# A convolution, norm and FFN kernel: interleaved partitions, another weight path, smaller first parts, a new order

## The chip, the cores and the metric

One core of a Trainium2 chip. The metric is the device time of one execution in microseconds; 921.21 us is the median of 3 runs of the kernel before (921.13 to 921.22).

## The reference

For x of 8 x 4224 x 192 and gate logits of 8 x 4224 x 8 x 7 (batch, position, head, tap):

```python
w = softmax(weight_gen, axis=-1)                        # 7 taps per head
x_unf = the 7 positions s-6 .. s of x, zeros before position 0
out = einsum('bshk,bskhg->bshg', w, x_unf)              # 24 channels per head
xn = (out - mean) / sqrt(var + 1e-6) * g_ln             # over 192 channels
result = out + maximum(xn @ w_ch1, 0) @ w_ch2           # 192 -> 768 -> 192
```

w_ch1 and w_ch2 arrive as float64; the other inputs and the result are float32.

## The kernel before

The 8 x 4224 positions are cut into 128 runs of 264; a partition holds one run, partition p the run p in order, so a batch takes 16 neighbouring partitions. A "token" is one column, 128 positions at once, and t runs from 0 to 263. The taps of the first six tokens need the six positions before the run: `load_x` (L277) fetches them into the columns 0 to 5 of the x buffer with one transfer for each batch (L286), and the first partition of each batch keeps zeros (L234). x lives in a ring of 36 columns.

Work goes by *parts* (`PARTS`, L21: three of 4 tokens, twenty of 12, then 8 and 4), cut into *chunks* of 4 or 6 tokens. For a part, `softmax` (L303) makes the tap weights in PSUM (wn). For a chunk, `conv` (L350) has VectorE multiply x by the weights (L382): three instructions with two taps each into pr, one with one tap into y. Two accumulating transfers issued by GpSimd (L388) and four GpSimd additions (L385) sum the taps; in the first chunk VectorE adds instead. `norm` (L416) has ScalarE make sums and squares of each token (L426, L431), the reciprocal root for the whole part (L454), five small VectorE steps (L459 to L465), and then for each *group* of four tokens the scaled activation (L477), its float16 high half (L484, ScalarE) and low half (L486, GpSimd), and a transposing transfer from SyncE's queue into xT (L490).

`products` (L494) takes a group. In each of three *hidden blocks* ten matmuls of 128x512 (L505) fill one ph in PSUM; ScalarE takes the Relu's high half (L514), VectorE its low half (L516). `output` (L525) makes the second product, 18 matmuls of 128x192 for each token (L537 to L539) into po, and VectorE adds two tokens to y (L550), which then goes out (L557). There are two each of ph, po, hh and hlo.

The weights come first. Their float64 words are loaded from SyncE's queue (L578; the last 64 rows of W1 twice, into both halves of the partitions). `from_double` (L592) joins two 32-bit words into a float32 with three VectorE steps (L611, L614, L617), through a second tile half in pr, and GpSimd flushes tiny values to zero (L621, L622). `w_scale` (L628) finds a power of two from the sum of squares through a matmul with ones (L633). W1 is scaled by g and split into a high and low float16 half; its last 64 rows and shifted copies lie in further blocks, copied by ScalarE (L683) and VectorE (L697). W2 is converted in two halves; its final scale is fs (L708), its halves are made at L714 (ScalarE) and L716 (GpSimd).

The order is planned ahead: each operation has an engine, an estimated cost and a due time in tokens (`WANT`, `W_WANT`, L29: so many tokens ahead of the group's turn on TensorE), and `Plan.order` (L88) places operations one after another on a model of the engines; it takes, among those that can start within `AHEAD` ns of the first, the one due first, and only those due within `WINDOW` tokens of the oldest open one. `FIRST` shifts the first 12 tokens. Each engine then works through its list in that fixed order, SyncE's and GpSimd's transfers included.

Of the kernel before, what the change touches and what calls it, by code (L numbers as in the profile page):

```python
# [20 lines left out]
PARTS = (4, 4, 4) + (12,) * 20 + (8, 4)  # L21
# [7 lines left out]
WANT = {'load': 30, 'wload': 43.75, 'max': 23.72, 'sub': 26.56, 'exp': 24.37, 'sum': 21.85,  # L29
    'rcp': 21.33, 'inv': 20.83, 'mul': 15.95, 'conv': 18.52, 'step': 0.9, 'dma': -0.4, 'add':  # L30
    0.61, 'sums': 6.45, 'squares': 6.1, 'rstd': 5.09, 'newton': 3, 'xh': 1.38, 'lo': 5.87}
W_WANT = {'load': 38.65, 'a': 20.41, 'c': 19.78, 's1': 14.01, 'load2': 16.96, 'c2': 6.55, 's2':
    5.13}
FIRST = {'soft': 1.35, 'conv': -1.66, 'norm': 6.53}
AHEAD = 57.45
WINDOW = 8
# [14 lines left out]
class Plan:  # L51


    DMA_START = {"SP": 1250.0, "Pool": 650.0}
# [101 lines left out]
def kernel(  # L156
# [21 lines left out]
    PMAX = max(PARTS)  # L178
    MMAX = PMAX * H
    assert sum(PARTS) == C and D == 192 and F == 6 * P and S == PB * C  # L180

# [11 lines left out]
    pool("w", 3, [P, PMAX, HK], F32)  # L193
# [35 lines left out]
    def dma_ns(n):  # L229
        return n * P / 350.0  # L230
# [3 lines left out]
    Q.memset(X[:, 0:PAD, :], 0.0)  # L234
# [8 lines left out]
    xsrc = xf.rearrange("(p t) d -> p t d", p=P)  # L243
    wsrc = wg.rearrange("b s h k -> (b s) (h k)").rearrange("(p t) f -> p t f", p=P)
    osrc = out.rearrange("b s d -> (b s) d").rearrange("(p t) d -> p t d", p=P)

    parts, chunks, s0 = [], [], 0
    for n in PARTS:
        pa = dict(S=s0, n=n, chunks=[], xT={})
        o = 0  # L250
        while o < n:
            m = min(CHUNK, n - o) if n % CHUNK == 0 else min(4, n - o)
            ch = dict(S=s0 + o, o=o, n=m, part=pa)
# [13 lines left out]
    def pieces(ch, k):  # L267

        t0, n = ch["S"], ch["n"]
        if t0 % RING == 0:  # L270
            return t0 % RING + k
        return xcol(t0) - PAD + k

    def sp(want, fn, r, w, dma):
        op("SP", 60, want, fn, r=r, w=w, dma=dma)

    def load_x(ch):  # L277
        t0, n = ch["S"], ch["n"]
        want = t0 - WANT["load"]
        if t0 == 0:  # L280

            def first():
                for b in range(B):
                    p = b * PB + 1
                    src = bass.AP(tensor=xf.tensor, offset=(p * C - PAD) * D, ap=[[C * D, PB - 1], [1, PAD * D]])
                    SY.dma_start(X[p : p + PB - 1, 0:PAD, :].rearrange("p t d -> p (t d)"), src)  # L286
            op("SP", 480, want, first, w=[("x", "h")], dma=dma_ns(PAD * D * 4))
        elif t0 % RING == 0:
            sp(want, lambda: SY.dma_start(X[:, 0:PAD, :], xsrc[:, t0 - PAD : t0, :]), [], [("x", "h")],
               dma_ns(PAD * D * 4))  # L290
# [125 lines left out]
    def norm(pa):  # L416
# [53 lines left out]
        for g in range(0, n, NT):  # L470
# [9 lines left out]
            for j in range(0, NT, 2):  # L480
# [10 lines left out]
               [(hl, 0), (hl, 1)], [xT], 2300.0)  # L491


    def products(pa, g, s, prev):  # L494
# [13 lines left out]
        for u in range(3):  # L508
# [3 lines left out]
            op("PE", 2160, su, lambda u=u, ph=ph: hidden(u, ph), [xT, "w1"], [ph])  # L512
# [12 lines left out]
    def output(gp, t, s):  # L525
# [28 lines left out]
        for ch in pa["chunks"]:  # L554
            if ch["y"] is y and j + 2 == ch["n"]:
                n, t0 = ch["n"], ch["S"]
                sp(s + 0.4, lambda: SY.dma_start(osrc[:, t0 : t0 + n, :], at(y)[:, :n, :]),  # L557
                   [(y, i) for i in range(n)], [], dma_ns(n * D * 4))
# [3 lines left out]
    for name, shape, dt in (("g", [P, 2], F32), ("gi", [P, 2], F32), ("s1", [P, 4], F32),  # L562
# [3 lines left out]
        W[name] = cp.tile(shape, dt, name="c_" + name)  # L566
    gcol = g_ln.rearrange("(d o) -> d o", o=1)
    hn = NF // 2 * D
# [6 lines left out]
    def load_weights():  # L575

        def dma(want, dst, src, n, w):
            op("SP", 60, -W_WANT[want], lambda: SY.dma_start(dst(), src), w=[w], dma=dma_ns(n))  # L578
# [5 lines left out]
        dma("load2", lambda: words(2, 0, 2 * NF * D).rearrange("p (j d) -> p j d", d=2 * D), wv2,  # L584
            8 * NF * D, raw[2])

    def load_g():
        A.dma_start(W["g"][:, 0:1], gcol[0:P, :])
        for h in (top, bot):
            A.dma_start(W["g"][h, 1:2], gcol[P:D, :])  # L590

    def from_double(want, src, dst, n, sq, r, w):  # L592


        m = Buf("pr")
        t = m
# [4 lines left out]
        def mv():  # L601
            return at(m)[:, 0].rearrange("p t d -> p (t d)")[:, :n]

        def tv():
            return at(t)[:, 1].bitcast(I32).rearrange("p t d -> p (t d)")[:, :n]

        want = -W_WANT[want]
        op("ACT", a_ns(n), want, lambda: A.activation(mv(), part(1).bitcast(F32), AF.Square), r, [(m, 0)])

        op("V", v_ns(n / 2), want,  # L610
           lambda: V.tensor_scalar(out=tv(), in0=part(1), scalar1=3, scalar2=0x3FFFFFFF,  # L611
                                   op0=ALU.logical_shift_left, op1=ALU.bitwise_and), r, [(t, 1)])
        op("V", v_ns(n), want,
           lambda: V.scalar_tensor_tensor(out=tv(), in0=part(0), scalar=29, in1=tv(),  # L614
                                          op0=ALU.logical_shift_right, op1=ALU.bitwise_or), r, [(t, 1)])
# [9 lines left out]
        op("ACT", a_ns(n, 186), want,  # L625
           lambda: A.activation(mv(), dst(), AF.Square, accum_out=sq), w, [(m, 0), (w[0], "sq")])
# [25 lines left out]
    def weights():  # L652
# [5 lines left out]
        def f32(b, n, o=0):  # L658
            if b is not w2r:
# [4 lines left out]
        from_double("c", lambda: words(1, 0, 2 * F), lambda: f32(wc, F), F, s1[:, 1:2],  # L664
                    [(raw[1], 0), (raw[1], 1)], [wc])
# [9 lines left out]
        op("V", 580, want, gsum, [(wa, "sq"), (wc, "sq")], ["s1"])  # L675
# [28 lines left out]
        op("V", 70, want2, lambda: V.tensor_tensor(out=s2[:, 2:3], in0=s2[:, 0:1], in1=s2[:, 1:2], op=ALU.add),  # L704
           [((w2r, 0), "sq"), ((w2r, 1), "sq")], ["s2"])
        w_scale("s2", s2[:, 2:3], 16384.0, r2, ["s2"], "r2")
# [4 lines left out]
        wv = [(w2r, 0), (w2r, 1)]  # L711
# [8 lines left out]
    load_g()  # L720
    for i, pa in enumerate(parts):
        load_w(pa)
# [5 lines left out]
        softmax(pa)  # L728
        for ch in pa["chunks"]:
            conv(chunks.index(ch))  # L730
# [39 lines left out]
```

## Time and profile before

| | |
|---|---|
| median of the runs | 921.21 us |
| profiled execution, its own time | 926.91 us |
| its span, first to last instruction | 925.1 us |
| busy share: TensorE, VectorE, ScalarE, GpSimd | 90%, 85%, 73%, 75% |
| mean granted TensorE clock | 0.989 |
| moved by transfers | 145.10 MB, 157 GB/s on average |

PE is TensorE, DVE is VectorE, ACT is ScalarE, POOL is GpSimd, SP is SyncE; a trailing q means the engine's queue, which also issues transfers. L12 is line 12 of the kernel. A timeline or chain row gives the start in us, the duration in us and what ran; a bracket gives the idle time before it and what ended it. The chain of waits is followed back from the last instruction.

### The profile page before, as it was taken

The page shows a single profiled execution, that of the slowest core. Times are in us where ns is not written, and L with a number is a line of the kernel's source. Part 1 is how long each engine was busy: PE and PEld are TensorE (multiplying, and loading weights), DVE is VectorE, ACT ScalarE, POOL GpSimd, SP SyncE. Part 2 cuts the span into 40 slices and gives each one's busy share as a digit, 9 for nine tenths or more (in the row PEclk, how much of TensorE's full clock was granted, in tenths as well). Part 3 has the DMA queues.
Part 4 walks back from the last instruction along what each step waited for, and adds up shares of the span by engine and source line. Part 5 has one row for each costly group of instructions (what it writes and reads, how often), then busy time and mean ns, then how long its engine had stood idle before and what let it go on. Part 6 is the DMA issues. An engine that isn't in the chain of part 4 may idle for free.

```text
span 925.1 us, 17424 instructions
## 1 busy us (share of the span) xinstructions
PE 831.6 (90%) x6736; PEld 588.4 (64%) x6736; DVE 790.6 (85%) x798; ACT 676.9 (73%) x1760; POOL 697.5 (75%) x378
## 2 busy tenths in 40 slices
PE   0025889999989999999999899999999999999998
PEld 0012647676767677777767677767776767777776
DVE  6989989988969889899898898988989889886432
ACT  2466779787777877968879578787796877878721
POOL 5688997977859788797887787978879688797200
PEclk9997989999999999999999999999999999999999
DMA  7446586798897898987987989889898798756311
GB/s 215 149 106 157 137 203 158 127 217 148 146 174 132 229 159 158 204 146 190 179 137 201 144 192 178 128 203 168 179 206 117 189 164 169 160 113 137 67 37 52
DMA packets 136018, 145.10 MB, mean 157 GB/s; under 512 B 107400, under 2 KB 108808, under 8 KB 135936
## 3 DMA queue, kind: packets, MB, share of 16 engines
q1 hardware_dynamic: 122672, 92.88, 44.6%
q0 software_dynamic: 12960, 51.12, 31.5%
q8 instruction: 52, 0.85, 0.4%
q14 instruction: 30, 0.25, 0.1%
q10 hardware_dynamic: 304, 0.00, 0.0%
HBM read 40.96 MB, written 25.95 MB: 72 GB/s over the span
## 4 chain that ended last, share of the span: by engine, by line
PE 64%; DVE 19%; DMA 7%; POOL 5%; issue 4%; ACT 1%; SPq 0%; DVEq 0%; POOLq 0%
PE ph L505 34%; PE po L539 10%; PE po L537 10%; PE po L538 10%; DVE pr L382 9%; DMA xT<-hl 6%; POOL y L385 4%; DVE hlo L516 3%; DVE y L382 2%; DVE y L550 1%; DMA hh<-in_moe_w_ch_dram 1%; POOL hl L486 1%; DVE y L385 1%; DVE pr L614 1%; DVE wn L343 1%
## 5 line engine op out<-in xcount | busy, mean ns | idle before, releaser
L385 POOL TENSOR_TENSOR y<-y,pr 128x1152 f32<-128x1152 f32 (+1 forms) x180 | 483.5, 2690 | 66.2 <-DVE pr L382 62.8
L505 PE MATMUL ph<-xT,c_w1h 128*128 128x512 f16 x1188 | 422.7, 384 | 53.8 <-DMA xT<-hl 43.5
L539 PE MATMUL po<-c_w2h,hlo 128*128 128x192 f16 x1584 | 389.8, 246 | 3.1 <-DVE hlo L516 3.1
L538 PE MATMUL po<-c_w2l,hh 128*128 128x192 f16 x1584 | 389.8, 246 | 0.7 <-POOL c_w2l L716 0.7
L537 PE MATMUL po<-c_w2h,hh 128*128 128x192 f16 x1584 | 389.8, 246 | 0.0
L382 DVE TENSOR_TENSOR pr<-x,wn 128x2304 f32<-128x2304 f32 (+1 forms) x138 | 334.8, 2439 | 2.8 <-POOL y L385 2.1
L514 ACT ACTIVATE hh<-ph 128x1024 f16<-128x1024 f32 x198 | 200.6, 1013 | 155.4 <-PE ph L505 155.4
L505 PE MATMUL ph<-xT,c_w1l 128*128 128x512 f16 x792 | 304.3, 384 | 0.0
L516 DVE SCALAR_TENSOR_TENSOR hlo<-ph,hh 128x1024 f16<-128x1024 f32 x198 | 240.6, 1216 | 60.7 <-ACT hh L514 60.6
L505 PEld LDWEIGHTS <-c_w1h 128*128 128x128 f16 x1188 | 117.6, 99 | 138.6 <-DMA xT<-hl 9.8
L486 POOL TENSOR_TENSOR hl<-xh,hl 128x768 f16<-128x768 f32 x66 | 113.8, 1725 | 86.9 <-ACT hl L484 81.5
L537 PEld LDWEIGHTS <-hh 128*128 128x128 f16 x1584 | 155.1, 98 | 22.6 <-issue 0.3
L538 PEld LDWEIGHTS <-hh 128*128 128x128 f16 x1584 | 155.1, 98 | 22.6 <-issue 0.3
L539 PEld LDWEIGHTS <-hlo 128*128 128x128 f16 x1584 | 155.0, 98 | 4.4 <-DVE hlo L516 3.5
L505 PEld LDWEIGHTS <-c_w1l 128*128 128x128 f16 x792 | 78.2, 99 | 111.9 <-POOL e L322 27.5
L477 ACT ACTIVATE xh<-y,s 128x192 f32<-128x192 f32 x264 | 125.7, 534 | 3.7 <-DVE s L465 3.7
L431 ACT ACTIVATE junk<-y,s 128x192 f32<-128x192 f32 x264 | 119.5, 453 | 6.6
L550 DVE SCALAR_TENSOR_TENSOR y<-po,c_fs,y 128x384 f32<-128x384 f32 x132 | 80.4, 609 | 47.8 <-PE po L539 47.8
L426 ACT ACTIVATE junk<-y 128x192 f32<-128x192 f32 x264 | 95.5, 362 | 26.5 <-POOL y L385 15.3
L388 POOL DMA_DIRECT2D pr<-pr x90 | 89.1, 993 | 12.8 <-DVE pr L382 6.6
L382 DVE TENSOR_TENSOR y<-x,wn 128x1152 f32<-128x1152 f32 (+1 forms) x46 | 59.4, 1292 | 0.1
L484 ACT ACTIVATE hl<-xh 128x768 f16<-128x768 f32 x66 | 55.3, 838 | 1.4
(63 smaller groups left out, 350.2 us busy)
## 6 DMA issues: line engine op xcount, KB each, us to landing
pr<-pr POOLq DMA_DIRECT2D x80, 576.0 KB, 7.5
x<-in_x_dram SPq DMA_DIRECT2D x47, 576.0 KB, 6.5
out_dram<-y SPq DMA_DIRECT2D x40, 576.0 KB, 7.5
w<-in_weight_gen_dram SPq DMA_DIRECT2D x20, 336.0 KB, 3.8
pr<-pr POOLq DMA_DIRECT2D x10, 384.0 KB, 4.1
x<-in_x_dram SPq DMA_DIRECT2D x6, 384.0 KB, 6.1
out_dram<-y SPq DMA_DIRECT2D x6, 384.0 KB, 2.7
pr<-in_moe_w_ch_dram SPq DMA_DIRECT2D x1, 1152.0 KB, 9.5
```

The costliest lines, as they stand in the source:

```text
L382: V.tensor_tensor(out=ov, in0=xv, in1=wv, op=ALU.mult)
L385: E.tensor_tensor(out=flat(0), in0=flat(0), in1=flat(k), op=ALU.add)
L426: A.activation(junk, at(y)[:, j, :], AF.Identity, scale=-1.0 / D, accum_out=at(s4)[:, 3, t : t + 1])
L431: A.activation(junk, at(y)[:, j, :], AF.Square, bias=at(s4)[:, 3, t : t + 1], accum_out=at(s4)[:, 0, t : t + 1])
L477: A.activation(at(xh)[:, t, :], at(y)[:, i, :], AF.Identity, bias=at(s4)[:, 3, g + t : g + t + 1], scale=at(s4)[:, 1, g + t : g + t + 1])
L486: lambda xh=xh, hl=hl: Q.tensor_tensor(out=at(hl)[:, :, 1, :], in0=at(xh), in1=at(hl)[:, :, 0, :], op=ALU.subtract),
L505: T_.matmul(at(ph)[:, v, :], w[:, wb, fsl], xv[:, xb, :, :], start=(i == 0), stop=(i == len(steps) - 1))
L514: lambda us=us, ph=ph: A.activation(at(hh)[:, us, :], at(ph), AF.Relu), [ph], [(hh, u)])
L516: lambda us=us, ph=ph: V.scalar_tensor_tensor(out=at(hlo)[:, us, :], in0=at(ph), scalar=0.0, in1=at(hh)[:, us, :], op0=ALU.max, op1=ALU.su ...
L537: T_.matmul(o, at(hh)[:, j, q], w2h[:, j, :], start=(j == 0), stop=False)
L538: T_.matmul(o, at(hh)[:, j, q], w2l[:, j, :], start=False, stop=False)
L539: T_.matmul(o, at(hlo)[:, j, q], w2h[:, j, :], start=False, stop=(j == NF - 1))
```

## The change

- Partition p holds block p // 8 of batch p % 8. The history columns then have the same form for all partitions but the first 8, and one transfer brings them; x, gate logits and output are addressed by `tokens`.
- W1's two loads and g's two are issued from ScalarE's queue, W1's last 64 rows once. The word joining uses PSUM (ph for W1, po for W2) in place of the second half of pr, the flush is a fourth VectorE step, W2 goes in three thirds.
- The shifted copies of W1 are four transfers from SyncE's queue. A hidden block waits for each piece of W1 by name.
- `PARTS` starts with six parts of 4 and six of 8. Softmax has parts of its own (`SOFT`).
- New due times, `AHEAD`, `WINDOW` and cost estimates for transfers.

```diff
-PARTS = (4, 4, 4) + (12,) * 20 + (8, 4)
+PARTS = (4,) * 6 + (8,) * 6 + (12,) * 15 + (8, 4)
+SOFT = (4, 8) + (12,) * 21
...
+WANT = {'load': 35.31, 'wload': 45.13, 'max': 23.73, 'sub': 26.8, 'exp': 29.21, 'sum': 19.41,
+    'rcp': 16.76, 'inv': 19.08, 'mul': 14.75, 'conv': 17.87, 'step': 0.85, 'dma': -0.4, 'add':
+    0.2, 'sums': 8.31, 'squares': 3.24, 'rstd': 5.29, 'newton': 6.27, 'xh': 1.75, 'lo': 6.1}
+W_WANT = {'load': 23.7, 'a': 23.19, 'c': 24.61, 's1': 21.01, 'load2': 14.54, 'c2': 3.68, 's2':
+    7.55}
+FIRST = {'soft': -1.12, 'conv': -1.17, 'norm': 7.8}
+AHEAD = 13.38
+WINDOW = 11.37
...
-        return n * P / 350.0
+        return n * P / 280.0
...
-    Q.memset(X[:, 0:PAD, :], 0.0)
+    Q.memset(X[0:B, 0:PAD, :], 0.0)
...
+    def tokens(ap, t0, n):
+        f = ap.shape[-1]
+        return bass.AP(tensor=ap.tensor, offset=t0 * f, ap=[[C * f, PB], [PB * C * f, B], [1, n * f]])
...
-        op("SP", 60, want, fn, r=r, w=w, dma=dma)
+        op("SP", 450, want, fn, r=r, w=w, dma=dma)
...
             def first():
-                for b in range(B):
-                    p = b * PB + 1
-                    src = bass.AP(tensor=xf.tensor, offset=(p * C - PAD) * D, ap=[[C * D, PB - 1], [1, PAD * D]])
-                    SY.dma_start(X[p : p + PB - 1, 0:PAD, :].rearrange("p t d -> p (t d)"), src)
+                src = bass.AP(tensor=xf.tensor, offset=(C - PAD) * D, ap=[[C * D, PB - 1], [PB * C * D, B], [1, PAD * D]])
+                SY.dma_start(X[B:P, 0:PAD, :].rearrange("p t d -> p (t d)"), src)
...
-        dma("load", lambda: words(0, 0, 2 * F), w1b[0:P, :], 8 * F, raw[0])
-        for i, h in enumerate((top, bot)):
-            dma("load", lambda h=h: words(1, 0, 2 * F)[h, :], w1b[P:D, :], 4 * F, (raw[1], i))
+        dma("ACT", A, "load", lambda: words(0, 0, 2 * F), w1b[0:P, :], 8 * F, raw[0])
+        dma("ACT", A, "load", lambda: words(1, 0, 2 * F)[top, :], w1b[P:D, :], 4 * F, raw[1])
+        dma("ACT", A, "load", lambda: W["g"][:, 0:1], gcol[0:P, :], 200, "g0")
+        dma("ACT", A, "load", lambda: W["g"][top, 1:2], gcol[P:D, :], 100, "g1")
...
-        m = Buf("pr")
-        t = m
+        m, t = Buf("pr"), Buf(space)
...
         op("V", v_ns(n), want,
-           lambda: V.scalar_tensor_tensor(out=dst().bitcast(I32), in0=part(1), scalar=-0x40000000, in1=tv(),
-                                          op0=ALU.bitwise_and, op1=ALU.bitwise_or), [*r, (t, 1)], w)
-        def flush():
-            Q.tensor_scalar(out=mv(), in0=mv(), scalar1=TINY * TINY, scalar2=None, op0=ALU.is_ge)
-            Q.tensor_tensor(out=dst(), in0=mv(), in1=dst(), op=ALU.mult)
-        op("Pool", 2 * q_ns(n), want, flush, [], [(m, 0), *w])
+           lambda: V.scalar_tensor_tensor(out=tv(I32), in0=part(1), scalar=-0x40000000, in1=tv(I32),
+                                          op0=ALU.bitwise_and, op1=ALU.bitwise_or), r, [t])
+        op("V", v_ns(n), want,
+           lambda: V.scalar_tensor_tensor(out=dst(), in0=mv(), scalar=TINY * TINY, in1=tv(F32),
+                                          op0=ALU.is_ge, op1=ALU.mult), [m, t], w)
...
+        def shift(dst, src, r, w):
+            op("SP", 450, want, lambda: SY.dma_start(dst, src), r, w, dma=dma_ns(F))
+        copy(lambda: w1h[:, 0, :], lambda: f32(wa, F), [wa, "gi"], ["h0"], gi[:, 0:1])
+        shift(w1h[bot, 1, :], w1h[top, 0, :], ["h0"], ["h1b"])
+        shift(w1h[top, 2, :], w1h[bot, 0, :], ["h0"], ["h2t"])
...
+        shift(w1h[bot, 2, :], w1h[top, 1, :], ["h1t"], ["h2b"])
...
+        shift(w1l[bot, 1, :], w1l[top, 0, :], ["l0"], ["l1b"])
...
-        op("V", 269, want, lambda: V.tensor_copy(out=w1l[bot, 1, :], in_=w1l[top, 0, :]),
-           ["l0", "l1t", "h1b", "h2b", "h2t", "h1t"], ["w1"])
-        for h in range(2):
-            from_double("c2", lambda h=h: words(2, 2 * h * hn, 2 * hn), lambda h=h: f32(w2r, hn, h * hn),
-                        hn, s2[:, h : h + 1], [raw[2]], [(w2r, h)])
+        tn = NF // 3 * D
+        for h in range(3):
+            from_double("c2", lambda h=h: words(2, 2 * h * tn, 2 * tn), lambda h=h: f32(w2r, tn, h * tn),
+                        tn, s2[:, h : h + 1], [raw[2]], [(w2r, h)], "po")
```

## Rows read from the trace of the kernel before

**Rows 1.** The page: span, and TensorE's busy time with its matmuls.

```profile
span 925.1 us, 17424 instructions
PE 831.6 (90%) x6736; PEld 588.4 (64%) x6736; DVE 790.6 (85%) x798; ACT 676.9 (73%) x1760; POOL 697.5 (75%) x378
```

**Rows 2.** The chain of waits, one group's distance in the middle: start, us, what.

```profile
301.11 2.16 PE ph L505 x10
...
313.53 2.16 PE ph L505 x10
```

**Rows 3.** Timeline of TensorE: first hidden block, wait for W2, last matmul.

```profile
60.79 0.58 PE L505 MATMUL ph<-xT,c_w1h 128*128 128x512 f16 x1 [34.74 <-DMA xT<-hl]
...
89.69 0.24 PE L538 MATMUL po<-c_w2l,hh 128*128 128x192 f16 x1 [0.66 <-POOL c_w2l L716]
...
920.38 0.25 PE L539 MATMUL po<-c_w2h,hlo 128*128 128x192 f16 x1
```

**Rows 4.** Stretch of the Relus (L514): stretch, length, ScalarE busy (count), clock, transfers.

```profile
0.00:90.80 90.80, 5.06 (x5) 0.94 0.61 160
```

**Rows 5.** Waits of TensorE: what it waited for, us in total, times, longest.

```profile
PE ph L505 <- DMA xT<-hl: 43.5, 6, 34.7
```

**Rows 6.** The chain of waits around 124 us.

```profile
123.79 7.35 PE ph L505 x20
```

**Rows 7.** Timeline of TensorE: the three late waits.

```profile
527.30 0.39 PE L505 MATMUL ph<-xT,c_w1h 128*128 128x512 f16 x1 [2.62 <-DMA xT<-hl]
...
602.61 0.39 PE L505 MATMUL ph<-xT,c_w1h 128*128 128x512 f16 x1 [0.64 <-DMA xT<-hl]
...
715.88 0.39 PE L505 MATMUL ph<-xT,c_w1h 128*128 128x512 f16 x1 [1.36 <-DVE hlo L516]
```

**Rows 8.** Stretches: busy us (instructions) of PE, PEld, DVE, ACT, POOL; clock, DMA share, GB/s.

```profile
10.00:89.00 79.00, 16.52 (x55) 6.91 (x56) 73.60 (x88) 43.04 (x110) 61.79 (x36) 0.94 0.61 160
89.00:262.00 173.00, 161.09 (x1306) 113.74 (x1304) 159.93 (x149) 135.93 (x369) 149.98 (x79) 0.98 0.78 157
300.00:500.00 200.00, 200.00 (x1648) 143.10 (x1646) 182.38 (x182) 160.94 (x420) 162.69 (x86) 1.00 0.89 179
```

**Rows 9.** Timeline: the end of W2's preparation on VectorE and GpSimd.

```profile
82.37 2.33 DVE L708 SCALAR_TENSOR_TENSOR c_fs<-c_r,c_r 128x1 f32<-128x1 f32 x1
...
87.27 2.38 POOL L716 TENSOR_TENSOR c_w2l<-hlo,c_w2h 128x1152 f16<-128x1152 f32 x1 [2.60 <-ACT c_w2h L714]
```

**Rows 10.** First 90 us, VectorE alone: lines L611, L614 and L617 in turn.

```profile
0.00:90.00 90.00, 4.04 (x4) 0.94 0.62 161
...
0.00:90.00 90.00, 6.20 (x4) 0.94 0.62 161
...
0.00:90.00 90.00, 4.38 (x4) 0.94 0.62 161
```

**Rows 11.** Groups by line and shape: count | busy us, mean ns | idle before.

```profile
L385 POOL TENSOR_TENSOR y<-y,pr 128x1152 f32<-128x1152 f32 x160 | 444.5, 2779 | 63.0 <-DVE pr L382 60.2
...
L382 DVE TENSOR_TENSOR pr<-x,wn 128x2304 f32<-128x2304 f32 x120 | 303.5, 2543 | 2.6 <-POOL y L385 2.1
...
L550 DVE SCALAR_TENSOR_TENSOR y<-po,c_fs,y 128x384 f32<-128x384 f32 x132 | 80.4, 609 | 47.8 <-PE po L539 47.8
...
L385 POOL TENSOR_TENSOR y<-y,pr 128x768 f32<-128x768 f32 x20 | 39.6, 1981 | 3.2 <-DVE pr L382 2.6
L382 DVE TENSOR_TENSOR pr<-x,wn 128x1536 f32<-128x1536 f32 x18 | 31.3, 1747 | 0.2
...
L697 DVE COPY c_w1l<-c_w1l 64x768 f16<-64x768 f16 x1 | 1.5, 1543 | 0.0
```

**Rows 12.** W1's first load (chain), history of x (timeline), W2's load (issues, us to landing).

```profile
1.65 8.45 DMA hh<-in_moe_w_ch_dram
...
4.50 9.93 SPq L286 DMA_DIRECT2D x<-in_x_dram  x8
...
pr<-in_moe_w_ch_dram SPq DMA_DIRECT2D x1, 1152.0 KB, 9.5
```

More of the change, by code (lines that the diff above doesn't have):

```diff
@@ L26 @@
 TINY = struct.unpack("<f", struct.pack("<I", (1023 - 126) << 20))[0]
[L29 to L36, printed above, removed]
+WANT = {'load': 35.31, 'wload': 45.13, 'max': 23.73, 'sub': 26.8, 'exp': 29.21, 'sum': 19.41,
[6 more added lines that the diff above has]
+WINDOW = 11.37
 class Buf:
@@ L177 @@
     PB = P // B
-    PMAX = max(PARTS)
-    MMAX = PMAX * H
-    assert sum(PARTS) == C and D == 192 and F == 6 * P and S == PB * C
+    PMAX, SMAX = max(PARTS), max(SOFT)
+    MMAX = SMAX * H
+    assert sum(PARTS) == sum(SOFT) == C and D == 192 and F == 6 * P and S == PB * C
     V, A, Q, T_, SY = nc.vector, nc.scalar, nc.gpsimd, nc.tensor, nc.sync
@@ L242 @@
     xf = x.rearrange("b s d -> (b s) d")
-    xsrc = xf.rearrange("(p t) d -> p t d", p=P)
-    wsrc = wg.rearrange("b s h k -> (b s) (h k)").rearrange("(p t) f -> p t f", p=P)
-    osrc = out.rearrange("b s d -> (b s) d").rearrange("(p t) d -> p t d", p=P)
+    def tokens(ap, t0, n):
+        f = ap.shape[-1]
+        return bass.AP(tensor=ap.tensor, offset=t0 * f, ap=[[C * f, PB], [PB * C * f, B], [1, n * f]])
+    wf = wg.rearrange("b s h k -> b s (h k)")
+    softs, s0 = [], 0
+    for n in SOFT:
+        softs.append(dict(S=s0, n=n))
+        s0 += n
     parts, chunks, s0 = [], [], 0
@@ L252 @@
             m = min(CHUNK, n - o) if n % CHUNK == 0 else min(4, n - o)
-            ch = dict(S=s0 + o, o=o, n=m, part=pa)
+            so = max((q for q in softs if q["S"] <= s0 + o), key=lambda q: q["S"])
+            assert s0 + o + m <= so["S"] + so["n"] and (s0 + o) // RING == (s0 + o + m - 1) // RING
+            ch = dict(S=s0 + o, o=o, n=m, part=pa, so=s0 + o - so["S"])
             chunks.append(ch)
@@ L556, in output @@
                 n, t0 = ch["n"], ch["S"]
-                sp(s + 0.4, lambda: SY.dma_start(osrc[:, t0 : t0 + n, :], at(y)[:, :n, :]),
+                sp(s + 0.4, lambda: SY.dma_start(tokens(out, t0, n), at(y)[:, :n, :].rearrange("p t d -> p (t d)")),
                    [(y, i) for i in range(n)], [], dma_ns(n * D * 4))
@@ L566 @@
         W[name] = cp.tile(shape, dt, name="c_" + name)
+    for name in ("g", "s1"):
+        V.memset(W[name], 0.0)
     gcol = g_ln.rearrange("(d o) -> d o", o=1)
-    hn = NF // 2 * D
     top, bot = slice(0, 64), slice(64, P)
@@ L601, in mv, with tv @@
         def mv():
-            return at(m)[:, 0].rearrange("p t d -> p (t d)")[:, :n]
-        def tv():
-            return at(t)[:, 1].bitcast(I32).rearrange("p t d -> p (t d)")[:, :n]
+            return at(m)[rows, 0].rearrange("p t d -> p (t d)")[:, :n]
+        def tv(dt):
+            a = at(t).rearrange("p a b -> p (a b)") if space == "ph" else at(t)
+            return a[rows].bitcast(dt)[:, :n]
         want = -W_WANT[want]
-        op("ACT", a_ns(n), want, lambda: A.activation(mv(), part(1).bitcast(F32), AF.Square), r, [(m, 0)])
@@ L610, in from_double @@
[L610 to L612 removed]
+        op("ACT", a_ns(n), want, lambda: A.activation(mv(), part(1).bitcast(F32), AF.Square), r, [m])
         op("V", v_ns(n), want,
[L614 to L615 removed]
+           lambda: V.tensor_scalar(out=tv(I32), in0=part(1), scalar1=3, scalar2=0x3FFFFFFF,
+                                   op0=ALU.logical_shift_left, op1=ALU.bitwise_and), r, [t])
@@ L706, in weights @@
-        w_scale("s2", s2[:, 2:3], 16384.0, r2, ["s2"], "r2")
+        op("V", 70, want2, lambda: V.tensor_reduce(out=s2[:, 3:4], in_=s2[:, 0:3], axis=AX.X, op=ALU.add),
+           [((w2r, h), "sq") for h in range(3)], ["s2"])
+        w_scale("s2", s2[:, 3:4], 16384.0, r2, ["s2"], "r2")
         op("V", 130, want2,
@@ L710, in weights @@
         w2f, w2g = (a.rearrange("p j d -> p (j d)") for a in (w2h, w2l))
-        wv = [(w2r, 0), (w2r, 1)]
+        wv = [(w2r, h) for h in range(3)]
         op("ACT", a_ns(NF * D, 186), want2,
@@ L717, in weights @@
            ["w2h", "fs", *wv], ["w2"])
-    load_g()
+    todo = list(softs)
     for i, pa in enumerate(parts):
-        load_w(pa)
+        now = [q for q in todo if q["S"] < pa["S"] + pa["n"]]
+        todo = todo[len(now) :]
+        for q in now:
+            load_w(q)
         for ch in pa["chunks"]:
@@ L727 @@
             weights()
-        softmax(pa)
         for ch in pa["chunks"]:
+            if now and now[0]["S"] <= ch["S"]:
+                softmax(now.pop(0))
             conv(chunks.index(ch))
```

58 lines of the change are left out of this document (23 added, 35 removed).

## The prediction

> **What bounds the kernel now.** I read the page first: TensorE is busy for 831.6 of 925.1 us [rows 1], so the question is what the other tenth is made of. Next the chain of waits, for the pace: in the undisturbed middle, hidden blocks follow one another so that three of them and four output steps, which is one group of four tokens, take 313.53 - 301.11 = 12.42 us [rows 2] (two further hidden blocks lie between). There are 66 groups, so TensorE needs 66 x 12.42 = 819.7 us at the least, and 105.4 us of the span are loss. The reader should see that nothing in the diff changes the matmuls: the change can only move this loss.
>
> Then TensorE's own timeline, for where the loss lies [rows 3]. The first hidden block starts at 60.79, after a wait for a transposed activation (xT). The output steps are held at 89.69 by the low half of W2, and the last matmul starts at 920.38 and ends at 920.6. Up to 90.8 ScalarE had made only five Relus, so five hidden blocks stood finished when the steady work began [rows 4]: 5 x 2.16 = 10.8 us of useful work in 89.7 us. So the **front** loses 78.9 us. From 89.7 to 920.6 there are 830.9 us for 819.7 - 10.8 = 808.9 us of work: 22.0 us of loss. The **tail** after 920.6 is 4.5 us. Sum: 78.9 + 22.0 + 4.5 = 105.4.
>
> The 22.0 us split in two. Three late waits of TensorE, 2.62 + 0.64 + 1.36 = 4.6 us, lie at 527, 603 and 716 [rows 7]. The remaining 17.4 us are the **ramp** from 90 to 262: mostly waits for xT (43.5 us in all, of which 34.7 are the first one, before the ramp) [rows 5], and matmuls at the lower clock after them; 20 matmuls at 123.79 took 7.35 us instead of 2 x 2.16 [rows 6], 3.0 us lost.
>
> Last, the stretches by engine [rows 8]. From 10 to 89 us VectorE is busy for 73.60 of 79.00: the front is VectorE's queue. In the ramp it is busy 159.93 of 173.00 and GpSimd 149.98. In the middle, TensorE is busy all the time, VectorE for 182.38 of 200, GpSimd for 162.69; per group of 12.42 us that is 11.3 and 10.1 us. VectorE is hardly faster than TensorE, so what TensorE waits for early on is made up slowly.
>
> **The change, part by part.**
>
> *Front, order and sizes.* Steady work starts when W2 is ready: VectorE writes the final scale at 82.37 and GpSimd the low half at 87.27 [rows 9]. Until the scale, VectorE had made the products of three 4-token chunks, one 6-token chunk and two pair products of the next: five wide pair products and one single. The new due times put W2's conversion (3.68 tokens ahead) behind the products of token 12 (17.87 ahead, less the early shift) and before those of token 16, so VectorE does four 4-token chunks first. In place of 5 x 2.54 + 1.27 (a single product taken as half a pair) = 14.0 us stand 3 x 1.75 + 0.87 = 6.1 us [rows 11]: **-7.9 us**. The copy L697, 1.54 us on VectorE [rows 11], becomes a transfer: **-1.5**.
>
> *Word conversion.* Before: 12 VectorE steps, 4.04 + 6.20 + 4.38 = 14.6 us [rows 10], and GpSimd's flush steps. After: 8 steps of 768 and 12 of 384, since the flush moves to VectorE. For 384 elements out of PSUM the nearest row is the output sum, 0.61 us [rows 11]; for 768 I scale up to twice less its fixed part, about 1.0 (between 0.61 and 1.22). 8 x 1.0 + 12 x 0.61 = 15.3: **+0.7**; bounds, with each step a third cheaper or a quarter dearer, 10.2 (-4.4) and 19.1 (+4.5). The flush leaves GpSimd, which only shortens the way from one conversion step to the next; I take nothing for it, and up to -5 as a bound, since W2's chain passed through GpSimd four times.
>
> *W1 from ScalarE's queue, less data.* W1's first load took 8.45 us from 1.65 on, and VectorE's conversion starts at its end [rows 12]. If a queue of its own let it come at the rate of W2's load (1152 KB in 9.5 us [rows 12]), 768 KB would take 6.3 us and issue about a microsecond earlier: -3. If all loads share one rate, it is at best the earlier issue, under 1 us. I take 0, because x now comes at the same time. The Trainium skill, DMA: Bandwidth & Descriptors, section "Issuing engines are not separate DMA queues", says that transfers started by different engines run on the same DMA engines and that a second issuer saves issue time alone. By that rule the term is 0 to -1, by separate queues -3; the overlapping loads in this trace cannot decide it.
>
> *Interleaved partitions.* The history columns of x become one transfer instead of eight, which held SyncE's queue for 9.93 us [rows 12]. Token data then come nine microseconds earlier, but VectorE is on W1 until about 18 in either kernel; cover: W1's conversion; without it, up to -9 for the first product. The same DRAM rows move in the same sizes, on other partitions: 0.
>
> *Shifted copies by transfer.* Four transfers on SyncE's queue, each waiting for its source, with x loads and W2's load queued behind. At a price between 2 and 9.5 us each (the latter is W2's whole load [rows 12]), W1 is complete at about 35 to 45 us; cover: the first xT, which starts TensorE at 60.79 now [rows 3] and would have to come 15 us earlier to be held up. 0.
>
> So W2 is ready 7.9 + 1.5 - 0.7 = 8.7, say **9 us earlier**: steady work from about 81.
>
> *Ramp.* In the old kernel a part has 12 tokens from the fourth part on, so all 12 must be through products, sums and squares before the first of its three groups can be scaled; that is where xT is late. Parts of 4 and then 8 tokens, up to token 72, shorten this. Against it: small chunks cost more. VectorE pays 6.1 us for four tokens, against 2/3 of 3 x 2.54 + 1.27, 5.9; GpSimd's adds 4 x 1.98 = 7.9, against 2/3 x 4 x 2.78 = 7.4 [rows 11]. That makes about 11.5 and 10.6 us per group, and one more short chain of rstd steps per part. Still under 12.42, but at the ramp's share (92% for VectorE) 11.5 becomes 12.5. I take half of the 17.4 off: **-8**; bounds -17.4 and 0.
>
> *Later.* From token 72 on sizes are as before, order new: 0, bounds -4.6 (the three waits) and the rival below.
>
> **Sum:** -9 - 8 = -17 us. The profiled execution took 926.91 us, its span 925.1; the median of the runs is 921.21, 5.7 lower. The difference of 17 is carried over to the median: **904 us**, span about 908. About 0.2% (2 us) is what can be told from no change.
>
> **Rivals.**
> 1. *The ramp gives nothing.* Small chunks load VectorE and GpSimd so that what the shorter parts bring is lost. For it: VectorE was at 92% in the ramp. Against: GpSimd loses its flush steps. 921.2 - 9 = 912 (909 to 917).
> 2. *The ramp vanishes*, and the late waits with it: 921.2 - 9 - 17.4 - 4.6 = 890 (887 to 897). For it: 300 to 500 shows what a lead is worth. Against: VectorE at 91% builds a lead slowly.
> 3. *Slower: late transposes in the middle.* The new order (a much smaller look-ahead, 13.38 for 57.45) lets the first xT of each 12-token part come late. There are 15 such parts. At the 2.62 us of the wait at 527 that is 39 us, less the 4.6 there now: 921.2 - 17 + 35 = 939. It decides against the change from (17 + 4.6) / 15 = 1.4 us per part. For it: this wait exists three times already, by 1.54 us on average. Against: none between 300 and 500.
> 4. *The front does not move* since W2 waits for something else (buffers, scale chain), and the ramp neither: 921.
>
> **Chances.** Forecast (897 to 909) 0.45; rival 1 0.20; rival 2 0.15; rival 3 0.14; rival 4 0.06. Two thirds of rival 4 lie within 0.2%, the rest above and below. Faster: 0.45 + 0.20 + 0.15 + 0.01 = 0.81; same 0.04; slower 0.15. The range leaves out rivals 3 and 4: 888 to 918, which also takes in the bounds of the conversion (-4.4, +4.5) and W1 (-3) about 904.
>
> **What would show it.** Front: the wait for W2's low half ends near 81 (right), or at 88 or later (wrong). Conversion: 20 VectorE steps of 15 us in sum, none of them on GpSimd. Ramp: TensorE's loss between its first output step and token 72 is 9 us; 17 or more speaks for rival 1, under 3 for rival 2. Middle: TensorE's waits for xT after 300 us sum to 5 at most; 15 or more is rival 3. SyncE: one history load of well under 2 us, and the first product not before 16 us. The prediction is wrong if the start of TensorE's steady work moves by less than 4 us or more than 16, or if the pace of 12.42 does not hold.

## The result and the profile after

The changed kernel takes **909.98 us** (median; 907.79 to 914.2) against 921.17 us for the kernel before beside it: a ratio of 0.9885, 95% interval 0.9847 to 0.9924. It is 11.2 us faster; 17 were forecast, and the time lies in the range, though above the forecast's own 897 to 909. The profiled execution took 914.20 us with a span of 912.4, 12.7 less than before [rows 1].

The page of the kernel after: span and the engines' busy times, to be held against [rows 1].

```profile
span 912.4 us, 17537 instructions
PE 831.8 (91%) x6736; PEld 587.2 (64%) x6736; DVE 788.4 (86%) x837; ACT 667.1 (73%) x1766; POOL 689.9 (76%) x398
```

TensorE's 831.8 us are those of before, so the whole gain is loss taken away, as the prediction's ledger supposes. ScalarE is busy for 9.8 us less than before, GpSimd for 7.6 and VectorE for 2.2.

TensorE's timeline after, front: the first hidden block, the first one held by VectorE's low half, the first output step.

```profile
57.65 0.59 PE L506 MATMUL ph<-xT,c_w1h 128*128 128x512 f16 x1 [30.43 <-DMA xT<-hl]
...
69.33 0.59 PE L506 MATMUL ph<-xT,c_w1h 128*128 128x512 f16 x1 [4.58 <-DVE hlo L517]
...
76.45 0.25 PE L538 MATMUL po<-c_w2h,hh 128*128 128x192 f16 x1
```

Before, the output steps began at 88.78 and were still held at 89.69 [rows 3]; now they begin at 76.45, 12.3 us earlier, though one hidden block fewer stands finished (four Relus have started by 76.65, in place of five [rows 4]).

The stretches after (columns as in [rows 8]), ramp and middle:

```profile
74.00:300.00 226.00, 217.79 (x1751) 152.64 (x1750) 215.49 (x239) 185.46 (x506) 208.16 (x132) 0.99 0.91 175
300.00:500.00 200.00, 196.25 (x1602) 138.74 (x1600) 182.07 (x171) 153.55 (x411) 159.33 (x85) 1.00 0.96 169
```

The second row is the surprise. In the middle, where TensorE had been busy for 200.00 of 200 us [rows 8], it is now busy for 196.25.

One measure serves for all kernels, those of the experiments below included: the start of the k-th of ScalarE's 198 Relus, one for each hidden block. The 54th stands for token 72, where the small parts end; at TensorE's pace [rows 2] 18 of them take 6 x 12.42 = 74.5 us.

| kernel | median us | ratio (95%) | 5th | 24th | 54th | 198th Relu, us |
|---|---|---|---|---|---|---|
| before | 921.17 | 1 | 89.8 | 181.6 | 310.8 | 911.8 |
| after | 909.98 | 0.9885 (0.9847-0.9924) | 81.3 | 165.9 | 295.0 | 898.6 |
| e1_runs | 931.76 | 1.0114 (1.0086-1.0142) | 79.1 | 165.2 | 292.5 | 916.6 |
| e2_before_inter | 925.37 | 1.0044 (1.0024-1.0063) | 88.4 | 183.4 | 308.3 | 910.6 |
| e3_old_parts | 926.72 | 1.0061 (1.0034-1.0087) | 81.8 | 178.2 | 308.6 | 909.9 |
| e4_old_order | 937.32 | 1.0170 (1.0145-1.0195) | 93.5 | 188.5 | 318.7 | 921.8 |
| f1_no_stores | 912.65 | 0.9901 (0.9861-0.9940) | 81.2 | 163.1 | 290.5 | 892.2 |
| f3_three_hl | 905.96 | 0.9837 (0.9808-0.9865) | 80.6 | 165.1 | 294.3 | 889.7 |
| g1_old_join | 928.43 | 1.0070 (1.0046-1.0093) | 92.2 | 180.9 | 309.1 | 913.0 |
| h1_g_from_sp | 909.02 | 0.9871 (0.9824-0.9919) | 78.6 | 162.9 | 291.3 | 893.5 |
| k1_three_hl_g | 904.98 | 0.9834 (0.9802-0.9866) | 78.0 | 163.7 | 292.2 | 888.3 |
| k2_runs_three_hl | 906.05 | 0.9838 (0.9806-0.9870) | 78.5 | 165.7 | 293.0 | 893.7 |
| k3_before_three_hl | 920.85 | 1.0007 (0.9978-1.0037) | 90.2 | 180.6 | 305.7 | 903.8 |
| k4_before_join | 922.92 | 1.0028 (1.0005-1.0052) | 88.0 | 182.7 | 306.4 | 905.6 |

The last four columns come from one profiled execution each. That of before lies 5.7 us above its kernel's median, that of after 4.2, so the columns place a loss to a few microseconds, and the ratios decide. Each ratio is to runs of before made beside that kernel; their medians are 920.06 to 921.74 us, and single runs range from 915.58 to 928.59, but for one of 1311.96 at a clock of 0.669, which is left out. By the 54th Relu the change has gained 15.8 us, near the 17 forecast. From there to the last, before takes 601.0 us and after 603.6, for an ideal of 8 x 74.5 = 596: nothing more is gained, and 2.6 us go back.

### The profile page after: what moved, and what is told of

It is laid out like the page before. It is cut to its first block, busy times and chain, and to the rows that moved or that the text cites. A ratio compares the mean times of both kernels' runs of the same rounds, so it can differ in the third digit from the quotient of the medians.

```text
span 912.4 us, 17537 instructions
## 1 busy us (share of the span) xinstructions
PE 831.8 (91%) x6736; PEld 587.2 (64%) x6736; DVE 788.4 (86%) x837; ACT 667.1 (73%) x1766; POOL 689.9 (76%) x398
## 3 DMA queue, kind: packets, MB, share of 16 engines
q1 hardware_dynamic: 123735, 91.70, 51.4%
## 5 line engine op out<-in xcount | busy, mean ns | idle before, releaser
L386 POOL TENSOR_TENSOR y<-y,pr 128x1152 f32<-128x1152 f32 (+1 forms) x200 | 490.1, 2488 | 75.5 <-DVE pr L383 67.7
L517 DVE SCALAR_TENSOR_TENSOR hlo<-ph,hh 128x1024 f16<-128x1024 f32 x198 | 241.3, 1219 | 81.6 <-ACT hh L515 81.3
L478 ACT ACTIVATE xh<-y,s 128x192 f32<-128x192 f32 x264 | 123.7, 535 | 39.6 <-DVE s L466 39.5
L487 POOL TENSOR_TENSOR hl<-xh,hl 128x768 f16<-128x768 f32 x66 | 118.3, 1792 | 40.7 <-ACT hl L485 39.6
L389 POOL DMA_DIRECT2D pr<-pr x100 | 100.0, 1003 | 20.7 <-DVE pr L383 19.8
L551 DVE SCALAR_TENSOR_TENSOR y<-po,c_fs,y 128x384 f32<-128x384 f32 x132 | 80.3, 608 | 12.7 <-PE po L540 12.7
L485 ACT ACTIVATE hl<-xh 128x768 f16<-128x768 f32 x66 | 55.1, 835 | 27.7 <-DMA xT<-hl 27.5
```

The lines of the kernel that those rows point to most:

```text
L386: E.tensor_tensor(out=flat(0), in0=flat(0), in1=flat(k), op=ALU.add)
L389: Q.dma_start(flat(to), flat(k), accum_op=ALU.add, max_dma_last_dim=CHUNK * D * 4)
L478: A.activation(at(xh)[:, t, :], at(y)[:, i, :], AF.Identity, bias=at(s4)[:, 3, g + t : g + t + 1], scale=at(s4)[:, 1, g + t : g + t + 1])
L487: lambda xh=xh, hl=hl: Q.tensor_tensor(out=at(hl)[:, :, 1, :], in0=at(xh), in1=at(hl)[:, :, 0, :], op=ALU.subtract),
L517: lambda us=us, ph=ph: V.scalar_tensor_tensor(out=at(hlo)[:, us, :], in0=at(ph), scalar=0.0, in1=at(hh)[:, us, :], op0=ALU.max, op1=ALU.su ...
```

## Experiments: each part taken back

**Partitions in runs again.** My first theory was that interleaving slows the loads and costs the middle.

```diff
-        return bass.AP(tensor=ap.tensor, offset=t0 * f, ap=[[C * f, PB], [PB * C * f, B], [1, n * f]])
+        return bass.AP(tensor=ap.tensor, offset=t0 * f, ap=[[C * f, P], [1, n * f]])
...
+                for b in range(B):
+                    p = b * PB + 1
...
```

> The changed kernel with the old partitions (partition p holds run p in order, eight history transfers); order, parts and weight path as changed. Theory A (interleaved rows make transfers slower: x 8.5 us to landing against 6.5 before, gate logits 8.6 against 3.8, transposes 8.1 against 6.1, and this takes back some 6 us between token 72 and 120): x and logits land as before, the SP queue's share falls from 51% to about 45%, the 18 Relus 55 to 72 take 74.5 to 75.5 us instead of 77.7, the runs lie within 1 us of each other, and the median is 902 to 905 unless the eight history transfers hold back the front by some us. Theory B (the new order and the small chunks cause the loss in the middle): the middle is as in the changed kernel, 908 to 912.

It fell: 931.76 us, 22 slower than after, all of it lost after the 54th Relu (624.1 us in place of 603.6). Yet the loads of x do land faster here without interleaving. From the page of e1, the queue of SyncE's transfers (packets, MB, share of the 16 engines' time) and two issues (count, KB each, median us from issue to landing):

```profile
q1 hardware_dynamic: 123840, 91.70, 45.7%
...
x<-in_x_dram SPq DMA_DIRECT2D x37, 576.0 KB, 6.9
...
xT<-hl SPq DMA_TRANSPOSE x66, 8.4
```

The same of after:

```profile
q1 hardware_dynamic: 123735, 91.70, 51.4%
...
x<-in_x_dram SPq DMA_DIRECT2D x37, 576.0 KB, 8.5
...
xT<-hl SPq DMA_TRANSPOSE x66, 8.1
```

For the same bytes the interleaved layout takes a larger share of the transfer engines, and the kernel is faster all the same. The share is larger in all three pairs of kernels that differ in the layout (52.0% in e2 against 44.6 in before, 51.2 in f3 against 46.7 in k2). The landing time is not: with a third buffer, below, x's 576 KB land in 8.9 us interleaved (f3) and in 10.2 us in runs (k2). What the layout is worth comes out in the next section.

**Interleaving alone, in the kernel before.**

```diff
-xsrc = xf.rearrange("(p t) d -> p t d", p=P)
+        return bass.AP(tensor=ap.tensor, offset=t0 * f, ap=[[C * f, PB], [PB * C * f, B], [1, n * f]])
```

> The kernel before with interleaved partitions and one history transfer, nothing else. Theory A: logits land in 8 us instead of 3.8, x in 8 to 9, the middle loses 5 to 15 us, 925 to 935, runs spread by several us. Theory B: the layout is free; the history issue saves nothing either since VectorE is on W1: 920 to 922.

925.37 us, slower by 0.44%. Under the old order the interleaving is worth nothing, and costs a little; where those 4 us lie, one profile does not show (its 198th Relu is even 1.2 us earlier than before's).

**Old part sizes.**

```diff
-PARTS = (4,) * 6 + (8,) * 6 + (12,) * 15 + (8, 4)
+PARTS = (4, 4, 4) + (12,) * 20 + (8, 4)
```

> The changed kernel with the old parts (4, 4, 4, then 12s), all else changed. If the small first parts are what gains in the ramp (forecast: 8 us; trace: about 3 between the fifth Relu and token 72), the first output step stays near 76 and the span grows by 3 to 8: 913 to 918. If the small chunks cost more on VectorE and GpSimd than they gain: 903 to 908.

926.72 us. The front stays (5th Relu 81.8), then the whole gain is lost in the ramp: the 54th comes at 308.6, 13.6 us later than in after. Under the new order the small parts are needed: with parts of 12 from token 12 on, TensorE waits 10.05 us for one xT at 118.46, where the longest such wait of after in the ramp is 1.98 us. Four waits of ScalarE for a buffer, 10.1 us in all, of the kind described in the next section, also fall before e3's 54th Relu; what each costs was not separated.

**Old order** (due times, look-ahead, window and the estimates for transfers).

```diff
-AHEAD = 13.38
-WINDOW = 11.37
+AHEAD = 57.45
+WINDOW = 8
...
```

> The changed kernel with the old due times, AHEAD, WINDOW and transfer estimates. If the order is what brings W2 forward (as the forecast's front term of 8 us had it): the first output step falls back to 85 to 89 and the time to 918 to 928. If the word joining and ScalarE's queue do it: the first output step stays at 76 to 80. Theory B: the loss in the middle (6 us) goes away; theory A: it stays or grows, since the old order assumes faster transfers.

937.32 us, the worst of all. TensorE's timeline in e4, its waits for the two halves of W2:

```profile
74.99 0.32 PE L538 MATMUL po<-c_w2h,hh 128*128 128x192 f16 x1 [6.24 <-ACT c_w2h L714]
...
79.95 0.32 PE L539 MATMUL po<-c_w2l,hh 128*128 128x192 f16 x1 [4.65 <-POOL c_w2l L716]
...
80.22 0.37 PE L538 MATMUL po<-c_w2h,hh 128*128 128x192 f16 x1
```

TensorE's first step with W2 comes even earlier than in after (74.99 against 76.45), but it has waited 6.24 us for it and waits 4.65 more for the low half. From 75 to 85 us the granted clock is 0.50, the lower of its two levels, so that a matmul which takes 0.25 us in after at 76.45 takes 0.37 here, and the 5th Relu comes at 93.5. What the waits and what the clock cost was not separated.

**Old word joining, under the new order; and the new joining, under the old one.**

```diff
-        m, t = Buf("pr"), Buf(space)
+        m = Buf("pr")
+        t = m
...
+        def flush():
+            Q.tensor_scalar(out=mv(), in0=mv(), scalar1=TINY * TINY, scalar2=None, op0=ALU.is_ge)
```

> The changed kernel with the word joining of before (second half of pr in place of PSUM, flush on GpSimd), all else as changed, due times too. If the joining in PSUM earns a part of the front: VectorE's steps beside GpSimd take up to 2 us again, GpSimd gets 16 us of flush back, the first output step comes 4 to 8 us later than 76.4 and the time is 914 to 922. If the order alone earns the front: 76 to 78 and 908 to 913.

The reverse edit in the kernel before, with W2 in three thirds:

```diff
-        m = Buf("pr")
-        t = m
+        m, t = Buf("pr"), Buf(space)
...
-        for h in range(2):
+        for h in range(3):
```

> The kernel before with the new word joining alone (PSUM for the words, flush as a fourth VectorE step, W2 in three thirds), old order and parts. If joining by itself brings W2 forward: the scale (82.4) and W2's low half (87.3) come 5 to 10 us earlier and the time is 911 to 917. If it does so only under the new order: 80 to 83 and 85 to 88, 918 to 923.

Neither gains alone: g1 takes 928.43 us with its 5th Relu at 92.2, k4 922.92. (g1 gets two of the 264 tokens wrong, but runs every instruction, so its time stands for the work.) In k4 W2 is ready 11 us earlier than in before [rows 9], and the 5th Relu comes only 1.8 us earlier. Timeline of k4, W2's scale and low half:

```profile
73.39 2.60 DVE L708 SCALAR_TENSOR_TENSOR c_fs<-c_r,c_r 128x1 f32<-128x1 f32 x1
...
75.94 2.37 POOL L716 TENSOR_TENSOR c_w2l<-hlo,c_w2h 128x1152 f16<-128x1152 f32 x1
```

TensorE's waits in k4 (us, times, longest):

```profile
PE ph L505 <- DVE hlo L516: 8.6, 3, 7.4
```

The low halves of the Relus, on VectorE, are then late by up to 7.4 us (the wait ends at 77.18). So in k4 the front waits for other work in VectorE's queue, not for W2. The order and the joining have to change together.

## Experiments: the loss in the middle

The forecast's rival 3 looked for late transposes in TensorE's own waits for xT. After 300 us those sum to 0.6 us, and ScalarE's waits show the loss instead (kernel after: what waited for what, us in total, times, longest; the first line from 300 us on):

```profile
PE ph L506 <- DMA xT<-hl: 0.6, 1, 0.6
...
ACT hl L485 <- DMA xT<-hl: 27.5, 14, 4.6
```

No row like the second exists in the kernel before. ScalarE wants to write the next part's normalized tokens into hl, and there are two hl buffers; the older one is still being read by its transpose. The kernel after at the longest of these waits, by start in us, duration, engine:

```profile
434.30 1.44 SPq L491 DMA_TRANSPOSE xT<-hl  x1
...
439.08 8.51 SPq L491 DMA_TRANSPOSE xT<-hl  x1
...
448.27 0.84 ACT L485 ACTIVATE hl<-xh 128x768 f16<-128x768 f32 x1 [4.64 <-DMA xT<-hl]
...
450.04 1.00 ACT L515 ACTIVATE hh<-ph 128x1024 f16<-128x1024 f32 x1
...
451.07 1.23 DVE L517 SCALAR_TENSOR_TENSOR hlo<-ph,hh 128x1024 f16<-128x1024 f32 x1 [3.27 <-ACT hh L515]
...
452.35 0.26 PE L540 MATMUL po<-c_w2h,hlo 128*128 128x192 f16 x1 [0.57 <-DVE hlo L517]
```

From top to bottom this is one chain. The transpose issued at 434.30 lands at 448.25, 14 us later, and ScalarE's copy into its buffer starts at 448.27; the issue of the next one holds SyncE's queue for 8.51 us of that. ScalarE stands 4.64 us for the buffer, with sums of squares and a Relu queued behind it; VectorE waits 3.27 us for that Relu; TensorE loses 0.57 us on the low half, and VectorE the start of its next products.

**A third hl buffer.** The order of all instructions stays as it is; only the buffers are dealt out among three.

```diff
-    for o in plan.order():
+    todo = plan.order()
+    plan.pools["hl"].append(third)
+    for i, b in enumerate(sorted(hls, key=lambda b: b.ops[0].start)):
+        b.slot = i % 3
+    for o in todo:
```

> The changed kernel in the same order with three hl buffers instead of two, so that ScalarE's high-half copy needn't wait for the transposing transfer before the last. Theory C: ScalarE's waits for xT (27.5 us) are nearly gone, TensorE's waits for the Relu's low half (9.3 + 5.4) fall by half outside the front, the time falls by 3 to 7 us. Theory B: no change beyond 2 us.

905.96 us. Its runs (904.55 to 907.15) all lie below those of after (907.79 to 914.2). ScalarE's wait is gone from the list, and the pace is back; f3 in the middle (columns as in [rows 8]):

```profile
300.00:500.00 200.00, 200.00 (x1643) 142.77 (x1641) 188.47 (x182) 157.24 (x425) 166.04 (x88) 1.00 0.96 175
```

From the 54th to the last Relu f3 takes 595.4 us, the ideal of 596. The third buffer is worth 4.0 us in the median here, and 4.0 again between h1 and k1 below.

**Is it the buffer alone, or what the layout costs?** The same edit in e1 (k2) and in the kernel before (k3):

> The changed kernel with the old partitions and three hl buffers. Theory D (the old partitions cost 22 us in the changed order only through ScalarE's waits for the transposing transfer before the last; the layout itself is worth little): ScalarE's waits for xT vanish, the 18 Relus fall from 78 to 81 to about 75, time 904 to 910. Rival (the layout slows something else in the middle): 78 per 18 Relus stay, 925 or more.

> The kernel before with three hl buffers, its own order. Its late waits (2.62, 0.64, 1.36 us) and the wait at 262 stand behind a transposing transfer that itself starts late. If ScalarE's wait for the buffer makes it late: 4 to 6 us are gained, 915 to 917. If the low half on GpSimd or the transfer's own time makes it late: within 2 us of 921.

k2 takes 906.05 us: 25.7 less than e1, and what f3 takes. So with two buffers the layout is worth 22 us, with three nothing that can be told. Its worth lies in this wait, which in e1 is the longer one. ScalarE's waits in e1:

```profile
ACT hl L487 <- DMA xT<-hl: 49.1, 14, 5.1
```

The middle in k2 (columns as in [rows 8]), nearly full again; in these profiles k2 is 1.3 us ahead of f3 at the 54th Relu and takes 5.3 us longer from there on:

```profile
300.00:500.00 200.00, 198.28 (x1627) 141.30 (x1625) 185.88 (x174) 156.69 (x423) 162.65 (x86) 1.00 0.94 176
```

k3 takes 920.85 us (0.9978 to 1.0037): the kernel before has no use for a third buffer. It is the new order that brings the wait: e4, which has all of after but the order, shows no wait of ScalarE for hl either. Which part of the order does it (due times, look-ahead, window or estimates) was not tried.

**Are the output's stores what delays the transposes?**

```diff
+                def store():
+                    if t0 + n == C:
+                        SY.dma_start(tokens(out, t0, n), at(y)[:, :n, :].rearrange("p t d -> p (t d)"))
```

> The changed kernel without its output transfers, but for the last chunk's (left out: 50 of 51 stores, 25.6 MB of 145; order unchanged). Theory C (the middle waits for transposing transfers that share the transfer engines with accumulating transfers, loads and stores; two high-half copies on ScalarE wait for them, the Relus behind these come late, and TensorE waits): transposes land in 6 us or less instead of 8.1, ScalarE's waits for xT (27.5 us) fall below 10, the 18 Relus 55 to 72 take 75 us or less instead of 77.7, the span falls by 5 to 9. Theory B (VectorE's and GpSimd's work in the new order is the limit): the Relus keep 77, the span moves by less than 2.

No. f1 leaves out every store but the last chunk's. It takes 912.65 us, and although the share of the transfers that SyncE issues fell from 51.4 to 42.2% of the 16 engines' time, ScalarE's wait in f1 is nearly that of after:

```profile
ACT hl L485 <- DMA xT<-hl: 26.4, 14, 3.4
```

What makes the transposes late stays open. Their median from issue to landing in 300 to 620 us is 4.8 us in e4, under the old order, 10.8 in after and 12.8 in e1; with a third buffer it is no shorter (11.0 in f3, 13.2 in k2), but ScalarE no longer waits for it.

## Experiments: ScalarE's queue in the front

In the kernel after, g's two small loads stand on ScalarE's queue behind W1's. Timeline of after:

```profile
6.17 5.67 ACTq L580 DMA_DIRECT2D c_g<-in_moe_g_ln_dram  x2
...
11.89 0.39 ACT L326 ACTIVATE e<-e 128x224 f32<-128x224 f32 x1 [9.87 <-DMA x<-in_x_dram]
14.29 3.42 DVE L383 TENSOR_TENSOR pr<-x,wn 128x1536 f32<-128x1536 f32 x2
```

The trace puts the 9.87 us to a load of x, which the exponential does not read. The issue of g's loads, until 11.84, is the better reading, and moving them tests it:

```diff
-        dma("ACT", A, "load", lambda: W["g"][:, 0:1], gcol[0:P, :], 200, "g0")
+        dma("SP", SY, "load", lambda: W["g"][:, 0:1], gcol[0:P, :], 200, "g0")
```

> The changed kernel with g's two loads on SyncE's queue instead of ScalarE's; W1 stays on ScalarE's. In the changed kernel g's issue holds ScalarE from 6.17 to 11.84, and the first exponential stands behind it. If this hold costs the front: the exponential at about 7.5, the first product at about 10 to 11 instead of 14.3, the first output step 2 to 4 us earlier, the time 905 to 908. If x lands no earlier than 13 or the conversions set the front: first product at 13 to 14, no change.

Timeline of h1:

```profile
7.66 0.39 ACT L326 ACTIVATE e<-e 128x224 f32<-128x224 f32 x1 [5.64 <-POOL e L323]
...
11.76 3.42 DVE L383 TENSOR_TENSOR pr<-x,wn 128x1536 f32<-128x1536 f32 x2 [0.15 <-DMA x<-in_x_dram]
```

The exponential starts 4.2 us earlier, the first product 2.5, the 5th Relu 2.7. The time, 909.02 us (905.63 to 912.87), cannot be told from 909.98. This edit and f3's together:

> The changed kernel with three hl buffers and g's loads on SyncE's queue. The two alone gave 4 us in the middle (the 18 Relus 73 to 90 in 74.0 us instead of 77.4) and 2.5 to 3 us at the front (first Relu at 61.9 instead of 64.4). If they are independent: first Relu near 62, the middle at 74 to 75 per 18 Relus, 902 to 904. If the earlier front is waited away in the ramp: 905 to 906 as with three buffers alone.

904.98 us (901.09 to 908.67), the lowest median, 15 us under the runs of before beside it; its interval (0.9802 to 0.9866) covers that of f3, so g's share is not shown.

## Why the prediction was right, and where it was off

The time lies in the stated range, but in the window of rival 1 (909 to 917) and not in the forecast's own. Rival 1's mechanism is not what happened, for the ramp did gain. In the profiles, up to the last Relu, the three terms -9, -8 and 0 came out as -10.2, -5.6 and +2.6, -13.2 in sum in place of -17; so the front's extra gain made up for a part of what the other two missed, which is luck. The medians moved by 11.2.

**Front, -9: right in size, by other terms.** Output steps 12.3 us earlier, less the one hidden block not yet done (2.16), is 10.2. VectorE reaches W2's scale at 69.19 in place of 82.37 [rows 9], 13.2 us earlier. Up to there it was busy for 69.02 us before and 55.66 after, and idle for as long in both (13.4 and 13.5); the rows that differ most, from VectorE's groups of before up to 82.37 (count, busy us, mean ns, idle before):

```profile
L382 DVE TENSOR_TENSOR pr<-x,wn 128x1536 f32<-128x1536 f32 (+1 forms) x14 | 28.3, 2033 | 2.2 <-POOL y L385 2.1
L385 DVE TENSOR_TENSOR y<-y,pr 128x768 f32<-128x768 f32 x4 | 7.2, 1809 | 0.0
```

The same groups of after, up to 69.19:

```profile
L383 DVE TENSOR_TENSOR pr<-x,wn 128x1536 f32<-128x1536 f32 x14 | 24.2, 1744 | 0.2
L386 DVE TENSOR_TENSOR y<-y,pr 128x768 f32<-128x768 f32 x4 | 4.8, 1195 | 0.0
```

The pair products gave 4.1 us, and the single ones 0.4 (4.2 to 3.8), in place of the 7.9 forecast: there are 14 pair products in either kernel, only narrower ones now, where I had counted fewer. Adds on VectorE gave 2.4 us that I had not counted, and one low half less gave 1.2. That the sum came out near 9 is luck.

**Joining, +0.7: -0.8 measured.** The 20 steps took 3.46 + 3.47 + 3.47 + 3.43 = 13.8 us, where 15.3 were forecast and before's twelve took 14.6 [rows 10]; one of the four lines in after (stretch, length, VectorE busy with count):

```profile
0.00:90.00 90.00, 3.46 (x5) 0.96 0.78 179
```

Its worth under the new order is not in this sum: g1, without it, is 18 us slower. There VectorE's steps take 18.0 us, GpSimd's flush 16.9, and TensorE waits 5.7 us for W2's high half; which of these decides was not separated.

**W1's queue, 0: right for the time, not for the load.** W1's first 768 KB landed 4.6 us after issue, in place of the 8.45 us of before [rows 12]; the first logits, 112 KB, took 5.3 us in place of 2.4, and the first maximum ran at 6.12 in place of 3.19. DMA issues of after:

```profile
hh<-in_moe_w_ch_dram ACTq DMA_DIRECT2D x1, 768.0 KB, 4.6
...
w<-in_weight_gen_dram SPq DMA_DIRECT2D x1, 112.0 KB, 5.3
```

VectorE took the first products (14.29) ahead of W1's conversion (17.63), so W1's early landing shortened nothing. The forecast sign, no product before 16 us, was wrong. The Trainium skill, DMA: Bandwidth & Descriptors, section "Issuing engines are not separate DMA queues", says that a second issuer saves only the time that issuing takes, since all run on the same engines. Between the two traces W1's load gained more than that, 3.8 us (with 1152 KB of W1 issued in place of 1536), and the logits lost 2.9: the shared engines fit, the issue time alone does not, for the single load.

**History and shifts, 0 each: as forecast, as far as the trace shows.** The one history load took 1.02 us to issue, the shifts landed in 2.1 us each (2 to 9.5 allowed), under the first xT's cover. Neither was tried alone.

**Ramp, -8: -5.6 measured.** From the first output step to the 54th Relu it went from 222.0 to 218.6 us, with 2.16 us more of hidden work: 5.6 off the 17.4, about 12 left. Between rival 1's 17 and the forecast's 9 it is nearer to the forecast. But under the new order the part sizes are worth more, 13.6 us (e3), since without them the ramp would be longer than before's: 226.8 us from the 5th to the 54th Relu, 221.0 in before and 213.7 in after.

**Later, 0: the term that was mis-sized.** It is +2.6 us in the profiles; with the third buffer it is 595.4 - 601.0 = -5.6, about its bound of -4.6. The step that failed is "sizes are as before, order new: 0": under the new order ScalarE waits 27.5 us for one of two hl buffers, a wait that the prediction did not have. Rival 3 had the place, a late transpose once per 12-token part (14 times here), but the wrong waiter, TensorE; through ScalarE it cost (603.6 - 595.4) / 14 = 0.6 us per part, against f3, under the 1.4 from which it decides. (One of the three waits that the rival built on, at 715.88, is for VectorE's low half and not for xT [rows 7].) By the sign that I had set, xT waits of 5 us at most after 300 us, the middle looked sound (0.6 us) while the pace of 12.42 did not hold: the 18 Relus after the 54th took 77.7 us. That clause of the prediction's failure test was met, though the time stayed in the range. It was a loose test: before itself has 18 Relus in 77.3 us, from the 90th to the 108th, around its wait at 527 [rows 7].

## What to carry to other kernels

After an edit to the order, read the waits of every engine for buffers, not only those of the bound engine: a copy that waits for a buffer holds all that is queued behind it. The buffer that a transfer reads came free only when the transfer had landed (448.25, the copy at 448.27), so count buffers by landing times. Parts of a change can be worthless one by one and needed together (joining and order), or worth 22 us only while another limit stands (layout and two buffers), so take each back from both sides.

## What the runs showed of the hardware

Two issues of 0.75 KB in all held ScalarE's instruction stream for 5.67 us (6.17 to 11.84) behind two loads on the same queue; with them moved to SyncE the exponential ran 4.2 us earlier.

The issue of a transpose held SyncE's queue for 1.44 us in one case and 8.51 in the next, behind a transpose still under way. From issue to landing a transpose took 3.4 to 15.4 us between 300 and 620 us, with a median of 10.8.

VectorE's first joining step, 768 words of 32 bits, took 4.24 us for two instructions into SBUF: 0.55 us for the first, and 3.77 us for the second, on half the partitions, while GpSimd was adding (18.07 to 21.73). Timeline of g1:

```profile
17.91 4.24 DVE L610 TENSOR_SCALAR pr<-hh 128x768 int32<-128x768 int32 x2
```

Into PSUM, beside the same kind of add, it took 1.80 us. Timeline of after:

```profile
17.63 1.80 DVE L610 TENSOR_SCALAR ph<-hh 128x768 int32<-128x768 int32 x2
```

With GpSimd idle, one such instruction takes 0.56 us into SBUF in the kernel before (at 10.12) and 0.96 us into PSUM in k4 (at 6.72), so in these runs PSUM was the dearer place for it alone and the cheaper one beside GpSimd.
